# Attention feeding a mixture of experts on one core: token rows in three buffers, scatters spread over more steps, and three products of zeros

## The chip, the core and the metric

The kernel runs on one core of a Trainium2 chip. The metric is the device time of one execution in microseconds. TensorE (PE) does matmuls and transposes, VectorE (DVE), ScalarE (ACT) and GpSimd (POOL) elementwise work; POOL and SyncE (SP) issue the DMA transfers.

## What is computed

The core of the reference:

```python
scores = scale * np.matmul(q, k.transpose(0, 1, 3, 2))          # 8 batches, 8 heads, 576 positions, 64 wide
# heads 0-3: (rel >= 0) & (rel < 32); heads 4-7: (rel >= 0) & same position modulo 32
attn = softmax(np.where(masks, scores, -1e9))
x = (attn @ v) as 4608 tokens x 512
logits = x @ w_gate + modality_bias[modality_id]                # 8 experts
e_idx = np.argmax(logits, axis=1)
gate_w = probs[np.arange(N), e_idx]
for e in range(8):
    mask = e_idx == e
    h = np.maximum(x[mask] @ w1[e], 0.0)                        # 512 x 1024
    out[mask] = gate_w[mask, None] * (h @ w2[e])                # 1024 x 512
```

## The kernel before

**Attention.** The work is cut into 32 units, `Local` (one of heads 0 to 3 for two batches) and `Strided` (two of heads 4 to 7 for one batch) in turn, eight units to each pair of batches `bp` (0 to 3, 1152 tokens each). A loop over steps `n` works on several units at once: in step n it loads unit n+3, computes the scores of unit n (`s` or `ss` on PE), transposes the softmax of unit n−2 (`turn`: `t`, `ts`) and multiplies unit n−3 by its values (`values`: `o` with `vv`, `ot` with `vs`). PE's instructions stand in the order in which the code is written there. The other engines, and everything in the expert part, are ordered by a scheduler.

**Routing.** When the last unit of a pair has its values, `finish_pair` and `route` are put into the list `extra` and advanced a few pieces a step (`pop`): transposes `xl` and `xs`, logits `lg`, the chosen expert `ohb`, running counts `cum` and `cnt`, and with `rk` and `ct` on PE each token's place in a table sorted by expert. The pair's token rows `xt` (128 × 9 rows of 528 words; the last 16 hold the token's number, its gate and padding) are then written to the table `xd` in DRAM by nine indirect DMAs from POOL, the scatters `xd<-xt,posi` (L646). These stand in the list `calm`, of which each call of `slow()` issues one. `slow()` is called after the scores in odd steps, after `turn` in every step, and after `values` in odd steps. A scatter is `paced`: it waits for the matmul or transpose that was newest on PE when it was written. Behind the scatters of pair 1 stands `early()`, which fetches, one piece a call, half of slot 0's weights (`raw<-in_w`, L811), its tokens in two halves (`fx<-xd`, L792), and then the same of slot 1.

**Experts.** 18 slots of 256 tokens of one expert and a half slot follow, some 23 us each. A slot has eight parts f: the weights' high halves `wh` are cast on ACT, the low halves `wl` computed on DVE, then come 12 products `h` (`xh`, `xl` with `wh`, `wl`) and, some parts later, the products `o`; `hh` (ACT) and `hl` (DVE) stand between, `y` is the gated output on ACT. Slot 0's tokens are transposed on PE ahead of the end of the attention; those of later slots by DMA (`cols`), after which `split_tokens` copies them into order (`xs`, two copies on DVE) and makes `xh` on ACT and `xl` on DVE. In slot k the split for slot k+1 is written at part f = SPLIT = 5. In slots 0 and 1 the routing of the last pair runs along.

**Memory.** The pools `ap`, `pre` and `lp` lie on the left. `xt` has two buffers by turns, so that pair 2 writes where pair 0's rows were.

Of the kernel before, what the change touches and what calls it, by code (L numbers as in the profile page):

```python
# [11 lines left out]
F32 = mybir.dt.float32  # L12
F32R = mybir.dt.float32r
# [7 lines left out]
P = 128  # L21
# [5 lines left out]
DM = H * D  # L27
# [6 lines left out]
NSLOT = NT // SLOT + E - 1  # L34
NSTATIC = 18
ROW = DM + 16
WARM = 10
SETUP = 6, 9
POPS, MIDS, POPF = 5, 2, 2
LT, RK = 7, (10, 5)  # L40
LAG = 2
# [152 lines left out]
def attention_moe(ctx: ExitStack, tc: tile.TileContext, a, out):  # L194
# [97 lines left out]
    pre = pre_cm.__enter__()  # L292
    lp_cm = tc.tile_pool(name="lp", bufs=2, reuse_waits="tile")
    lp = lp_cm.__enter__()
    pools["lp"] = lp


# [151 lines left out]
    class Strided:  # L449
# [49 lines left out]

        def turn(self):  # L500
            n = self.n
            tp = pa(f"ts{n}").rearrange("p (g q) -> p g q", g=4)
            for g in range(4):
                turned_to(tp[0:72, g, :], self.en[:, 4 * g:4 * g + 4, :])
            self.eb = eb = lp.tile([72, 16, 4, 18], F32, tag="eb", name=f"eb{n}")
            src = tp[0:72].rearrange("p g (u x) -> p (g u) x", u=4)[:, :, 0:18]
            sh = [72, 16, 2, 18]
            nc.vector.tensor_tensor(
                eb[:, :, 0:2, :], src.unsqueeze(2).to_broadcast(sh),
                cf[0:72, C_T:C_T + 2].unsqueeze(1).unsqueeze(3).to_broadcast(sh), ALU.mult)  # L510
            for t in (2, 3):
                nc.scalar.activation(eb[:, :, t, :], src, AF.Copy, scale=cf[0:72, C_T + t:C_T + t + 1])
# [52 lines left out]
    def route(bp, xt, xcs):  # L565
# [58 lines left out]
        sm = ap.tile([P, 9], F32, tag="sml", name=f"sml{bp}")  # L624
        nc.vector.tensor_reduce(sm[:], lo[:], AX.X, ALU.add)
        nc.vector.tensor_scalar(sm[:], sm[:], 1e-9, None, ALU.add)
        nc.gpsimd.memset(xt[:, :, DM + 2:ROW], 0.0)
        paced(nc.vector.tensor_copy(xt[:, :, DM].bitcast(I32), tok[:, 9 * bp:9 * bp + 9]))
        nc.vector.reciprocal(xt[:, :, DM + 1], sm[:])

# [187 lines left out]
        return xt  # L818

    def turn_half(xt):  # L820
        xs = pre.tile([P, 4, SLOT], F32R, tag="xh", name="xhh").bitcast(F32)[:, :, 0:P]
        t = pa("xth").rearrange("p (c q) -> p c q", c=4)
        for c in range(4):
            turned_to(t[:, c, :], xt[:, 0, P * c:P * c + P])
        nc.scalar.copy(xs, t)
        le = pre.tile([P, 2, 2], I32, tag="le", bufs=4, name="leh")
        nc.vector.tensor_copy(le[:, 0, :].bitcast(U16), xt[:, 0, DM:DM + 2].bitcast(U16))
        return le, xs
# [41 lines left out]

    def turn_tokens(n, xt):

        xh = pre.tile([P, 4, SLOT], F32R, tag="xh", name=f"xh{n}")
        xl = pre.tile([P, 4, SLOT], F32R, tag="xl", name=f"xl{n}")
        for c2 in range(2):
            t = pa(f"xt{n}{c2}").rearrange("p (c h q) -> p c h q", c=2, h=2)
            for c in range(2):
                for h in range(2):
                    cc = 2 * c2 + c
                    turned_to(t[:, c, h, :], xt[:, h, P * cc:P * cc + P])  # L880
            t = t.rearrange("p c h q -> p c (h q)")
            nc.scalar.copy(xh[:, 2 * c2:2 * c2 + 2, :], t)
            nc.vector.tensor_tensor(xl[:, 2 * c2:2 * c2 + 2, :], t, xh[:, 2 * c2:2 * c2 + 2, :].bitcast(F32), ALU.subtract)
        return xh, xl, entries(n, xt)
# [17 lines left out]
    def split_tokens(fp, n, cols, le):  # L902
        xs = fp.tile([P, 4, SLOT], F32, tag="xs", bufs=1, name=f"xs{n}")
        for w in range(2):
            dst = halves(xs)[:, :, :, w].rearrange("p c (h q) -> p c h q", h=2)
            pin(nc.vector.tensor_copy(dst, cols[:, :, w].rearrange("p h c q -> p c h q")))
        xh = pre.tile([P, 4, SLOT], F32R, tag="xh", name=f"xh{n}")
        xl = pre.tile([P, 4, SLOT], F32R, tag="xl", name=f"xl{n}")
        for c0 in (0, 2):
            c = slice(c0, c0 + 2)  # L910
            nc.scalar.copy(xh[:, c, :], xs[:, c, :])  # L911
            nc.vector.tensor_tensor(xl[:, c, :], xs[:, c, :], xh[:, c, :].bitcast(F32), ALU.subtract)  # L912
        return xh, xl, le
# [52 lines left out]


    units, ends = [], {}
    for bp in range(NBP):
        xt = ap.tile([P, 9, ROW], F32, tag="xt", bufs=2, name=f"xt{bp}")  # L970
        xcs = [ap.tile([P, T2], F32, tag=f"xc{c}", bufs=1 if c < 2 else 2, name=f"xc{bp}{c}") for c in range(4)]
        for i in range(4):
            units.append(Local(bp, i, xt))
            units.append(Strided(2 * bp + i // 2, i % 2, xcs[2 + i % 2]))
        ends[len(units) - 1] = (bp, xt, xcs)
# [12 lines left out]

    def early():
        for k in range(2):  # L990
            yield
            pin(paced(weights(tables[0][1], 0, k)))
            yield
            n, t, i, xrows = plan[k]
            for xt, ins in token_halves(n, tables[t][0], i, xrows):
                gathered[k] = xt
                pin(paced(ins))
                yield

    def slow():  # L1000
        while calm and next(calm[0], calm) is calm:
# [43 lines left out]
    for n in range(nu + 3):  # L1045
        if n + 3 < nu:
            units[n + 3].load()
        if 1 <= n <= nu:
            units[n - 1].load_values()
        if 2 <= n <= nu + 1 and not n % 2:  # L1050
            units[n - 2].spread_values()
        if n < nu:
            units[n].scores()
            if n % 2:
                slow()
            pop(MIDS)
        if 2 <= n <= nu + 1:
            units[n - 2].turn()
        slow()
        if n + 1 < nu:  # L1060
            units[n + 1].masks()
        if n >= 3:
            units[n - 3].values()
            if n - 3 in ends:
                extra.append(after(*ends[n - 3]))
        if n in SETUP:
            next(setup)
        if n >= nu or n % 2:
            slow()
        pop(POPS - MIDS if n < nu else POPS)  # L1070
        if n == nu + 1:
            turn(0)
    while calm:
        slow()
# [8 lines left out]
    for k, (n, *_) in enumerate(plan):  # L1083
        def between(f):
            pop(POPF)
            if f in DRIP:
                slow()
            if k + 1 < len(plan):
                if f == SPLIT:
                    turned[k + 1] = split_tokens(fp, plan[k + 1][0], *sent[k + 1])  # L1090
            elif f == 3:
                turn(k + 1)
            if not k and not f:
                gather(2)
            if f == FETCH:
                gather(k + 3)
            for at, m in ((SEND, 2),) if k else ((1, 1), (4, 2)):
                if f == at and k + m < len(plan):
                    sent[k + m] = send_tokens(fp, plan[k + m][0], gathered[k + m])

        ffn(fp, n, *turned[k], between, partial(load, k + 1))
# [20 lines left out]

    rest(plan[-1][2] + 1)
    fp_cm.__exit__(None, None, None)
    pre_cm.__exit__(None, None, None)
    ap_cm.__exit__(None, None, None)

# [17 lines left out]
```

## Time and profile before

| | |
|---|---|
| median of 3 runs | 600.34 us (600.19 to 600.82) |
| profiled execution | 597.48 us: span 595.4, and 2.08 around it |
| mean granted TensorE clock | 0.977 |
| busy, share of the span | PE 564.8 us (95%), DVE 426.1 (72%), ACT 358.7 (60%), POOL 244.7 (41%) |
| attention, up to some 158 us | PE busy 60.14 us of the first 73, 21.02 of 73 to 98, 29.92 of 98 to 131, 25.13 of 131 to 158 |

The span is what the profiler saw on the core, from the first instruction to the last. A share of busy time is a mean over the two parts of the kernel, which have little in common; a wait is read in its own place. "issue" as the cause of a wait means that the engine waited for nothing that the profile shows.

### The profile page before, as it was taken

Reading aid. Unit: us, or ns where it says so; the run is one execution under the profiler, and the core shown is the slowest. Engines: PE = TensorE matmul, PEld = TensorE weight load, DVE = VectorE, ACT = ScalarE, POOL = GpSimd, SP = SyncE. Lnnn points to the kernel's source line nnn. Section 1 sums busy time; section 2 is a strip of 40 time slices with the busy share of each in tenths; the row PEclk is TensorE's granted clock in tenths of the full one; section 3 lists DMA queues with packets and bytes.
Section 4 is the critical chain, followed back from the end, with each engine's and each line's share of the span. In section 5 each row is a group of like instructions: output and inputs, shape, how many; then the busy total and the mean of one; then the engine's idle time right before and its main releaser. Section 6 shows DMA issues by size and latency. Waiting matters only on the chain.

```text
span 595.4 us, 15277 instructions
## 1 busy us (share of the span) xinstructions
PE 564.8 (95%) x6040; PEld 494.4 (83%) x6040; DVE 426.1 (72%) x1050; ACT 358.7 (60%) x739; POOL 244.7 (41%) x219
## 2 busy tenths in 40 slices
PE   6979888989998999999999999999999999999995
PEld 3767776767887989999899899999998998998984
DVE  6776662957969997767767777777777677677541
ACT  3455664657866566666666666665665666666641
POOL 1413240143757786642543533533534533332220
PEclk9789997989999999999999999999999999999998
DMA  8988895897788855955934823413403438200621
GB/s 275 250 220 217 250 344 189 276 341 258 262 215 210 259 164 164 236 184 129 250 119 125 248 98 74 108 36 73 109 21 87 109 119 252 71 16 22 244 91 38
DMA packets 66669, 100.57 MB, mean 169 GB/s; under 512 B 47775, under 2 KB 49055, under 8 KB 63008
## 3 DMA queue, kind: packets, MB, share of 16 engines
q0 software_dynamic: 19744, 58.57, 29.7%
q1 hardware_dynamic: 46560, 40.56, 27.0%
q8 instruction: 49, 0.80, 0.6%
q10 hardware_dynamic: 288, 0.41, 0.2%
q14 instruction: 28, 0.23, 0.1%
HBM read 121.74 MB, written 19.43 MB: 237 GB/s over the span
## 4 chain that ended last, share of the span: by engine, by line
PE 85%; issue 5%; DVE 4%; DMA 3%; ACT 2%; POOL 1%; SPq 0%; POOLq 0%; ACTq 0%
PE h L924 33%; PE o L938 32%; PE o L420 3%; PE s L380 3%; PE ot L520 3%; PE lg L571 2%; PE xs L217 2%; PE t L217 2%; PE ss L476 1%; PE xl L217 1%; PE ts L217 1%; DMA vv<-in_vb 1%; ACT wh L959 1%; DVE wl L960 1%; DMA lqk<-in_qkl 1%
## 5 line engine op out<-in xcount | busy, mean ns | idle before, releaser
L960 DVE TENSOR_TENSOR wl<-raw,wh 128x512 fp32r<-128x512 f32 x288 | 185.9, 686 | 85.0 <-ACT wh L959 84.9
L959 ACT CAST wh<-raw 128x512 fp32r<-128x512 f32 x288 | 164.0, 618 | 91.4 <-PE o L938 89.6
L924 PE MATMUL h<-xl,wh 128*128 128x256 f32 x576 | 162.1, 282 | 1.4 <-DVE xl L912 1.4
L924 PE MATMUL h<-xh,wh 128*128 128x256 f32 x576 | 163.0, 284 | 0.2 <-ACT xh L911 0.2
L924 PE MATMUL h<-xh,wl 128*128 128x256 f32 x576 | 162.8, 283 | 0.0
L811 POOL DMA_INDIRECT raw<-in_w,wi x72 | 92.7, 1287 | 162.4 <-DVE wl L960 154.1
L924 PEld LDWEIGHTS h<-xl,wh 128*128 128x128 f32 x576 | 108.8, 189 | 8.1 <-DVE xl L912 2.1
L938 PE MATMUL o<-wh,hh 128*128 128x512 f32 x288 | 114.6, 398 | 0.0
L924 PEld LDWEIGHTS h<-xh,wh 128*128 128x128 f32 x576 | 108.4, 189 | 7.1 <-issue 0.6
L938 PE MATMUL o<-wl,hh 128*128 128x512 f32 x288 | 113.6, 395 | 0.0
L938 PE MATMUL o<-wh,hl 128*128 128x512 f32 x288 | 112.2, 395 | 0.0
L924 PEld LDWEIGHTS h<-xh,wl 128*128 128x128 f32 x576 | 108.3, 188 | 0.9
L927 ACT ACTIVATE hh<-h 128x256 fp32r<-128x256 f32 x144 | 55.2, 384 | 55.0 <-PE h L924 52.7
L929 DVE SCALAR_TENSOR_TENSOR hl<-h,hh 128x256 fp32r<-128x256 f32 x144 | 60.3, 419 | 12.5 <-ACT hh L927 12.3
L646 POOL DMA_INDIRECT xd<-xt,posi x36 | 40.4, 1121 | 59.1 <-DVE sms L496 16.5
L938 PEld LDWEIGHTS o<-wh,hl 128*128 128x128 f32 x288 | 53.7, 188 | 11.8
L938 PEld LDWEIGHTS o<-wh,hh 128*128 128x128 f32 x288 | 54.3, 188 | 7.6
L938 PEld LDWEIGHTS o<-wl,hh 128*128 128x128 f32 x288 | 54.3, 189 | 5.8
L946 POOL DMA_INDIRECT out<-y,le x36 | 46.2, 1283 | 24.0 <-ACT y L945 16.1
L792 POOL DMA_INDIRECT fx<-xd,li x36 | 39.2, 1090 | 23.6 <-issue 8.5
L409 ACT COPY et<-t 64x512 f32<-64x512 f32 x32 | 18.5, 579 | 21.1 <-PE t L217 20.7
L420 PEld LDWEIGHTS o<-vv,et 128*64 128x64 f32 x512 | 19.0, 152 | 13.4 <-issue 10.1
(183 smaller groups left out, 687.9 us busy)
## 6 DMA issues: line engine op xcount, KB each, us to landing
lqk<-in_qkl SPq DMA_DIRECT2D x32, 296.0 KB
sqk<-in_qks SPq DMA_DIRECT2D x32, 288.0 KB
vv<-in_vl SPq DMA_DIRECT2D x9, 520.0 KB
vs<-in_vs SPq DMA_DIRECT2D x16, 288.0 KB
raw<-in_w,wi POOLq DMA_INDIRECT x72, 2.5
vv<-in_vb SPq DMA_DIRECT2D x7, 146.2 KB
vv<-in_vb SPq DMA_DIRECT2D x7, 130.0 KB
vv<-in_vl SPq DMA_DIRECT2D x9, 65.0 KB
```

Source lines behind the costliest of these rows:

```text
L217: recent[:] = [nc.tensor.transpose(dst, src, ident)]
L420: recent[:] = [nc.tensor.matmul(os[bb][64 * jj:64 * jj + 64, bb + k, :], et[:, 2 * (k // 2) + bb, 2 * (k % 2) + jj, :, :].rearrange("p g q ...
L646: scattered(bp, paced(nc.gpsimd.indirect_dma_start(xd[0:(bp + 1) * T2, :], IOA(ap=posi[:, i:i + 1], axis=0), xt[:, i, :], None)))
L792: yield xt, fetches(min(xrows // T2, NBP) - 1, nc.gpsimd.indirect_dma_start(xt[:, h, :], None, xd[0:xrows, :], IOA(ap=li[:, s, h:h + 1], a ...
L811: return nc.gpsimd.indirect_dma_start(raws[j].rearrange("p f c -> p (f c)"), None, a["w"], IOA(ap=wi[:, s, j:j + 1], axis=0), bounds_check ...
L924: recent[:] = [nc.tensor.matmul(hp, w[:, a1], x[:, c, :], start=(k == 0), stop=(k == 11))]
L927: nc.scalar.activation(hh[:], hp, AF.Relu)
L929: nc.vector.scalar_tensor_tensor(hl[:], hp, 0.0, hh.bitcast(F32), ALU.max, ALU.subtract)
L938: nc.tensor.matmul(os[h], hx[:, m], w[:, 512:1024], start=(f == 0 and i == 0), stop=(f == 7 and i == 2))
L946: outs.add(nc.gpsimd.indirect_dma_start(out, IOA(ap=le[:, h, 0:1], axis=0), y[:], None, bounds_check=NT - 1, oob_is_err=False))
L959: nc.scalar.copy(wh[:, c], raw[:, c])
L960: nc.vector.tensor_tensor(wl[:, c], raw[:, c], wh[:, c].bitcast(F32), ALU.subtract)
```

## The change

```diff
--- before.py
+++ after.py
@@ -34,8 +34,9 @@
 NSLOT = NT // SLOT + E - 1
 NSTATIC = 18
 ROW = DM + 16
-WARM = 10
+WARM, FILL = 10, 3
 SETUP = 6, 9
+CALM = 27
 POPS, MIDS, POPF = 5, 2, 2
 LT, RK = 7, (10, 5)
 LAG = 2
@@ -292,6 +293,8 @@
     pre = pre_cm.__enter__()
     lp_cm = tc.tile_pool(name="lp", bufs=2, reuse_waits="tile")
     lp = lp_cm.__enter__()
+    sp_cm = tc.tile_pool(name="sp", side="right")
+    sp = sp_cm.__enter__()
     pools["lp"] = lp
 
 
@@ -499,7 +502,10 @@
 
         def turn(self):
             n = self.n
-            tp = pa(f"ts{n}").rearrange("p (g q) -> p g q", g=4)
+            bank = pa(f"ts{n}")
+            for _ in range(FILL if n == 0 else 0):
+                nc.tensor.matmul(bank, idle[:, 0:P], idle[:], start=True, stop=True)
+            tp = bank.rearrange("p (g q) -> p g q", g=4)
             for g in range(4):
                 turned_to(tp[0:72, g, :], self.en[:, 4 * g:4 * g + 4, :])
             self.eb = eb = lp.tile([72, 16, 4, 18], F32, tag="eb", name=f"eb{n}")
@@ -624,7 +630,6 @@
         sm = ap.tile([P, 9], F32, tag="sml", name=f"sml{bp}")
         nc.vector.tensor_reduce(sm[:], lo[:], AX.X, ALU.add)
         nc.vector.tensor_scalar(sm[:], sm[:], 1e-9, None, ALU.add)
-        nc.gpsimd.memset(xt[:, :, DM + 2:ROW], 0.0)
         paced(nc.vector.tensor_copy(xt[:, :, DM].bitcast(I32), tok[:, 9 * bp:9 * bp + 9]))
         nc.vector.reciprocal(xt[:, :, DM + 1], sm[:])
 
@@ -818,7 +823,7 @@
         return xt
 
     def turn_half(xt):
-        xs = pre.tile([P, 4, SLOT], F32R, tag="xh", name="xhh").bitcast(F32)[:, :, 0:P]
+        xs = pools["xp"].tile([P, 4, SLOT], F32R, tag="xh", name="xhh").bitcast(F32)[:, :, 0:P]
         t = pa("xth").rearrange("p (c q) -> p c q", c=4)
         for c in range(4):
             turned_to(t[:, c, :], xt[:, 0, P * c:P * c + P])
@@ -870,8 +875,8 @@
 
     def turn_tokens(n, xt):
 
-        xh = pre.tile([P, 4, SLOT], F32R, tag="xh", name=f"xh{n}")
-        xl = pre.tile([P, 4, SLOT], F32R, tag="xl", name=f"xl{n}")
+        xh = pools["xp"].tile([P, 4, SLOT], F32R, tag="xh", name=f"xh{n}")
+        xl = pools["xp"].tile([P, 4, SLOT], F32R, tag="xl", name=f"xl{n}")
         for c2 in range(2):
             t = pa(f"xt{n}{c2}").rearrange("p (c h q) -> p c h q", c=2, h=2)
             for c in range(2):
@@ -904,8 +909,8 @@
         for w in range(2):
             dst = halves(xs)[:, :, :, w].rearrange("p c (h q) -> p c h q", h=2)
             pin(nc.vector.tensor_copy(dst, cols[:, :, w].rearrange("p h c q -> p c h q")))
-        xh = pre.tile([P, 4, SLOT], F32R, tag="xh", name=f"xh{n}")
-        xl = pre.tile([P, 4, SLOT], F32R, tag="xl", name=f"xl{n}")
+        xh = pools["xp"].tile([P, 4, SLOT], F32R, tag="xh", name=f"xh{n}")
+        xl = pools["xp"].tile([P, 4, SLOT], F32R, tag="xl", name=f"xl{n}")
         for c0 in (0, 2):
             c = slice(c0, c0 + 2)
             nc.scalar.copy(xh[:, c, :], xs[:, c, :])
@@ -966,8 +971,11 @@
 
 
     units, ends = [], {}
+    xts = [(sp if i == 1 else ap).tile([P, 9, ROW], F32, bufs=1, name=f"xt{i}") for i in range(3)]
+    for t in xts:
+        nc.gpsimd.memset(t[:, :, DM + 2:ROW], 0.0)
     for bp in range(NBP):
-        xt = ap.tile([P, 9, ROW], F32, tag="xt", bufs=2, name=f"xt{bp}")
+        xt = xts[bp % 3]
         xcs = [ap.tile([P, T2], F32, tag=f"xc{c}", bufs=1 if c < 2 else 2, name=f"xc{bp}{c}") for c in range(4)]
         for i in range(4):
             units.append(Local(bp, i, xt))
@@ -988,14 +996,13 @@
 
     def early():
         for k in range(2):
+            n, t, i, xrows = plan[k]
+            for xt, ins in token_halves(n, tables[t][0], i, xrows):
+                yield
+                gathered[k] = xt
+                pin(paced(ins))
             yield
             pin(paced(weights(tables[0][1], 0, k)))
-            yield
-            n, t, i, xrows = plan[k]
-            for xt, ins in token_halves(n, tables[t][0], i, xrows):
-                gathered[k] = xt
-                pin(paced(ins))
-                yield
 
     def slow():
         while calm and next(calm[0], calm) is calm:
@@ -1051,7 +1058,7 @@
             units[n - 2].spread_values()
         if n < nu:
             units[n].scores()
-            if n % 2:
+            if n % 2 and n >= CALM:
                 slow()
             pop(MIDS)
         if 2 <= n <= nu + 1:
@@ -1069,6 +1076,9 @@
             slow()
         pop(POPS - MIDS if n < nu else POPS)
         if n == nu + 1:
+            sp_cm.__exit__(None, None, None)
+            xp_cm = tc.tile_pool(name="xp", bufs=2, side="right", reuse_waits="tile")
+            pools["xp"] = xp_cm.__enter__()
             turn(0)
     while calm:
         slow()
@@ -1086,7 +1096,7 @@
             if f in DRIP:
                 slow()
             if k + 1 < len(plan):
-                if f == SPLIT:
+                if f == (SPLIT if k else SPLIT - 1):
                     turned[k + 1] = split_tokens(fp, plan[k + 1][0], *sent[k + 1])
             elif f == 3:
                 turn(k + 1)
@@ -1122,6 +1132,7 @@
 
     rest(plan[-1][2] + 1)
     fp_cm.__exit__(None, None, None)
+    xp_cm.__exit__(None, None, None)
     pre_cm.__exit__(None, None, None)
     ap_cm.__exit__(None, None, None)
 
```

- **CALM = 27**: the call of `slow()` after the scores falls away in odd steps before 27. An odd step then issues two scatters in place of three, an even step one as before. Pair 0's nine, which took steps 15 to 19 (1, 1, 3, 1, 3), take steps 15 to 21 (1, 1, 2, 1, 2, 1, 1); pair 1's, steps 23 to 27 before, now end in step 28 (1, 1, 2, 1, 3, 1).
- **Three buffers**: `xt` of pair bp is `xts[bp % 3]`, and only pair 3 comes back to a buffer. The padding is set three times at the start, in place of once a pair in `route`. The second buffer lies in a pool on the right, closed at step 33; the pool `xp` then opened there takes `xh` and `xl`.
- **early()**: both halves of a slot's tokens go ahead of its weights.
- **FILL = 3**: three products of zeros, 128 × 512, into the PSUM bank of the first strided transposes `ts`, ahead of them (step 3).
- **SPLIT − 1** in slot 0: slot 1's tokens are split at part 4.

On POOL, where pairs 0 and 1 are scattered and the first slots are fetched, before (the number behind a name is its buffer; 1152x528 is the part of the table that a scatter can reach):

```order
L646 DMA xd<-xt_123,posi_1415 1152x528 x9
L627 MEMSET xt_133 128x9x14
L646 DMA xd<-xt_128,posi_2163 2304x528 x9
L627 MEMSET xt_138 128x9x14
L811 DMA raw_2704<-in_w,wi_2225 128x2048
L792 DMA fx_0_2787<-xd,li_2217 128x528 x2
L811 DMA raw_2904<-in_w,wi_2225 128x2048
L792 DMA fx_1_2975<-xd,li_2217 128x528 x2
L646 DMA xd<-xt_133,posi_2979 3456x528 x6
```
After:

```order
L651 DMA xd<-xt_126,posi_1422 1152x528 x9
L651 DMA xd<-xt_127,posi_2169 2304x528 x9
L797 DMA fx_0_2710<-xd,li_2223 128x528 x2
L816 DMA raw_2863<-in_w,wi_2231 128x2048
L797 DMA fx_1_2867<-xd,li_2223 128x528 x2
L816 DMA raw_3061<-in_w,wi_2231 128x2048
L651 DMA xd<-xt_128,posi_2981 3456x528 x7
```
Both memsets between the scatters are gone, and the weights `raw` have moved from ahead of two gathers to behind them; which step a scatter belongs to these rows don't show.

On PE at step 3, after the change (`ss` are the scores of the second strided unit, `s` the mask of the next local one):

```order
L472 MATMUL ss_292<-cb_sb 128x288
L479 MATMUL ss_292<-sqk_90 18x36 x32
L507 LDWEIGHTS idle
L507 MATMUL ts_343<-idle 128x512
L507 LDWEIGHTS idle
L507 MATMUL ts_343<-idle 128x512
L507 LDWEIGHTS idle
L507 MATMUL ts_343<-idle 128x512
L218 MATMUL ts_343<-cf_sb,ens_240 72x128 x4
L371 LDWEIGHTS cb_sb
L371 MATMUL s_355<-cb_sb 128x256
```
The six rows with `idle` are new; without them the `ts` transposes followed on the `ss` products.

On DVE towards the end of slot 0, before (the first digit behind `wl_` and `hl_` is the slot by turns, the second the part f):

```order
L610 TENSOR_TENSOR ohb_3502<-cf_sb,m_3500 128x72
L960 TENSOR_TENSOR wl_11_3719<-raw_2704,wh_11_3718 128x512
L625 TENSOR_REDUCE sml_3512<-lo_3491 128x9
L614 SCALAR_TENSOR_TENSOR cum_3504<-ohb_3502 128x72
L929 SCALAR_TENSOR_TENSOR hl_07_3589<-h_07_3574,hh_07_3587 128x256
L626 TENSOR_SCALAR sml_3512<-sml_3512 128x9
L616 TENSOR_TENSOR new_3506<-cum_3504,ohb_3502 128x8
L629 RECIPROCAL xt_138<-sml_3512 128x9
L906 COPY xs_1_3518<-cols_1_3338 128x1024
L617 TENSOR_TENSOR fst<-new_3506,cnt 128x8
L906 COPY xs_1_3518<-cols_1_3338 128x1024
L960 TENSOR_TENSOR wl_12_3762<-raw_2904,wh_12_3761 128x512 x2
```
After, the stretch behind `hl_07`:

```order
L934 SCALAR_TENSOR_TENSOR hl_07_3597<-h_07_3582,hh_07_3595 128x256
L610 TENSOR_TENSOR lo_3509<-lo_3509,mxl_3513 128x72
L965 TENSOR_TENSOR wl_12_3770<-raw_3061,wh_12_3769 128x512
L612 SCALAR_TENSOR_TENSOR sc_3516<-lo_3509,cf_sb 128x72
L965 TENSOR_TENSOR wl_12_3770<-raw_3061,wh_12_3769 128x512
L614 TENSOR_REDUCE m_3518<-sc_3516 128x9
L965 TENSOR_TENSOR wl_13_3809<-raw_3061,wh_13_3808 128x512 x2
L616 TENSOR_TENSOR ohb_3520<-cf_sb,m_3518 128x72
L631 TENSOR_REDUCE sml_3530<-lo_3509 128x9
L620 SCALAR_TENSOR_TENSOR cum_3522<-ohb_3520 128x72
L632 TENSOR_SCALAR sml_3530<-sml_3530 128x9
L622 TENSOR_TENSOR new_3524<-cum_3522,ohb_3520 128x8
```
The two copies of `xs` now stand 14 rows ahead of this piece, behind `hl_04`. `ohb` stood between the two halves of `wl_11` and stands behind `wl_13` now, and with it `cum`, `fst` and `cnt` have moved behind `wl_13` and `wl_14`.

On PE at the same place, before:

```order
L938 MATMUL o_01_3379<-wl_07_3566,hh_07_3587 128x512
L638 LDWEIGHTS cb_sb
L638 MATMUL rk_3594<-cum_3504,cb_sb 128x72
L938 MATMUL o_00_3378<-wh_07_3565,hl_07_3589 128x512
L938 MATMUL o_01_3379<-wh_07_3565,hl_07_3589 128x512
L924 MATMUL h_10_3612<-xh_1_3521,wh_10_3606 128x256
L692 LDWEIGHTS cb_sb
L692 MATMUL ct_3629<-cnt,cb_sb 128x32
L692 LDWEIGHTS cb_sb
L692 MATMUL ct_3629<-stp,cb_sb 128x32
L924 MATMUL h_11_3727<-xh_1_3521,wh_11_3718 128x256
L924 MATMUL h_12_3767<-xh_1_3521,wh_12_3761 128x256
```
After:

```order
L943 MATMUL o_01_3388<-wh_07_3573,hl_07_3597 128x512
L642 LDWEIGHTS cb_sb
L642 MATMUL rk_3602<-ohb_3520,cb_sb 128x72
L929 MATMUL h_10_3620<-xh_1_3459,wh_10_3614 128x256
L929 MATMUL h_10_3620<-xl_1_3460,wh_10_3614 128x256
```
and, nine products of `h_10` later:

```order
L929 MATMUL h_10_3620<-xh_1_3459,wl_10_3615 128x256
L643 LDWEIGHTS cb_sb
L643 MATMUL rk_3602<-cum_3522,cb_sb 128x72
L697 LDWEIGHTS cb_sb
L697 MATMUL ct_3637<-cnt,cb_sb 128x32
L697 LDWEIGHTS cb_sb
L697 MATMUL ct_3637<-stp,cb_sb 128x32
L929 MATMUL h_11_3735<-xh_1_3459,wh_11_3726 128x256
```
`rk<-ohb`, which stood among the products of part 6 and 7, is now the last thing ahead of slot 1's first product, and `rk<-cum` and both `ct` stand behind all 12 products of `h_10`, where `ct` stood behind the first.

## Rows read from the trace of the kernel before

**Rows 1.** Busy time by stretch (start:end, length, engines, clock, DMA share, GB/s).
```profile
191.00:595.00 404.00, 397.60 (x2533) 359.40 (x2531) 292.73 (x582) 244.91 (x482) 173.70 (x140) 1.00 0.45 128
```

**Rows 2.** PE's waits by line: us in total, times, longest.
```profile
PE o L420 <- issue: 7.4, 3, 4.0
PE ss L476 <- issue: 3.6, 4, 1.4
...
PE s L380 <- issue: 1.6, 1, 1.6
```

**Rows 3.** PE timeline: `lg` of bp 0, then step 19.
```profile
54.25 1.93 PE L571 MATMUL lg<-xc,wg_sb 128*32 128x256 f32 x32
...
86.40 0.68 PE L420 MATMUL o<-vv,et 128*64 128x65 f32 x15
91.06 1.24 PE L420 MATMUL o<-vv,et 128*64 128x65 f32 x17 [3.98 <-issue]
...
93.86 3.63 PE L571 MATMUL lg<-xc,wg_sb 128*32 128x256 f32 x32
```

**Rows 4.** The page's DMA queues over the whole run.
```profile
q8 instruction: 49, 0.80, 0.6%
```

**Rows 5.** DMA queues (packets, MB, share) in 82:88, 88:89 and 112:118 us.
```profile
q1 hardware_dynamic: 410, 1.29, 61.9%
q0 software_dynamic: 240, 0.81, 33.3%
...
q8 instruction: 1, 0.02, 5.9%
...
q1 hardware_dynamic: 418, 1.37, 80.8%
q0 software_dynamic: 62, 0.22, 9.2%
```

**Rows 6.** PE timeline at 110, at 121 and at the tokens of slot 0.
```profile
110.02 0.57 PE L476 MATMUL ss<-sqk 128*18 128x36 f32 x43 [0.37 <-issue]
...
121.07 1.24 PE L420 MATMUL o<-vv,et 128*64 128x65 f32 x21 [1.71 <-issue]
...
122.61 1.93 PE L380 MATMUL s<-lqk 128*32 128x128 f32 x32
...
153.96 1.09 PE L217 MATMUL xt<-cf_sb,fx 128*128 128x128 f32 x8
```

**Rows 7.** Busy time by stretch in two slow stretches, columns as in Rows 1.
```profile
16.00:22.00 6.00, 4.76 (x74) 3.85 (x76) 4.26 (x11) 0.89 (x2) 2.53 (x3) 0.50 0.94 271
...
91.00:97.00 6.00, 5.94 (x62) 3.71 (x66) 1.15 (x6) 0.76 (x2) 1.05 (x1) 0.50 0.71 249
```

**Rows 8.** POOL timeline: scatters, a memset and the last early gather.
```profile
85.38 0.96 POOL L646 DMA_INDIRECT xd<-xt,posi  x1 [2.03 <-PE xl L217]
...
97.02 0.20 POOL L627 MEMSET xt<- 128x126 f32 x1 [2.92 <-DMA xd<-xt,posi]
...
149.17 0.94 POOL L792 DMA_INDIRECT fx<-xd,li  x1 [0.86 <-PE ts L217]
```

**Rows 9.** PE timeline in the first 19 us.
```profile
1.87 3.96 PE L317 MATMUL warm<-idle 128*128 128x512 bf16 x10 [1.87 <-DVE idle L313]
...
15.10 0.74 PE L217 MATMUL ts<-cf_sb,ens 128*72 128x128 f32 x4 [1.02 <-DVE ens L498]
...
18.04 1.24 PE L420 MATMUL o<-vv,et 128*64 128x65 f32 x18 [0.57 <-POOL vv L361]
```

**Rows 10.** Timelines of PE, DVE and ACT between slots 0 and 1.
```profile
190.20 0.39 PE L924 MATMUL h<-xl,wh 128*128 128x256 f32 x1 [1.40 <-DVE xl L912]
...
176.35 1.29 DVE L960 TENSOR_TENSOR wl<-raw,wh 128x512 fp32r<-128x512 f32 x2 [1.20 <-ACT wh L959]
...
179.56 1.29 DVE L894 COPY rows<-fx 128x1024 uint16<-128x1024 uint16 x2 [1.10 <-issue]
...
188.05 1.25 ACT L945 ACTIVATE y<-o,le 128x512 f32<-128x512 f32 x2
```

## The prediction

> **What bounds the kernel now.** I read four views in this order: busy time by stretch, PE's waits, the PE timeline around the longest of them, and the DMA queues there. PE is the engine that ends last. From 191 us to the end, in the expert part, it is busy 397.60 of 404.00 us at full clock [rows 1], with the end of the output behind it, so nothing is to be had there. In the attention, ahead of 158 us, it waits more and doesn't always have the full clock. So the time that a change can win lies before 191 us, as PE's idle time or as time at half clock.
>
> The list of waits names "issue" for the most of PE's idle time: 7.4 us in three waits, 3.6 in four and 1.6 in one, 12.6 us on three lines [rows 2], where no semaphore holds PE. The longest is at step 19: PE runs 15 of 32 `o` matmuls from 86.40 to 87.08, and goes on at 91.06, 3.98 us later [rows 3]. What it lacked, the DMA view suggests: a queue of kind "instruction" (q8, 49 packets, 0.80 MB in the run, so 16 KB each [rows 4]) moves nothing in 82 to 88 us, and one packet of 0.02 MB in 88 to 89, two microseconds before PE resumes [rows 5]. I read these stalls as PE waiting for its next block of instructions, which stands in the DMA engines behind data. In 82 to 88 the engines are full: loads (q1) hold 61.9%, the indirect scatters and their like (q0) 33.3%. Before the 1.71 us stall that ends at 121.07 [rows 6], in 112 to 118, q0 held 9.2% and q1 80.8% [rows 5]. The loads are there both times; the scatters tell the two apart.
>
> The stall costs twice. From 91 to 97 PE is busy 5.94 of 6.00 us at a granted clock of 0.50, the 1.2 GHz level [rows 7]: its 32 `lg` matmuls take 3.63 us, where bp 0's took 1.93 at full clock [rows 3].
>
> The Trainium skill ("Runtime: NRT & Kernel Launch", Instruction fetch mechanics) says that the sequencer fetches its next page over its own DMA queue while it runs the current one, and that crossing a 16 KiB boundary is mostly hidden. By that page these waits would be something else and fewer scatters would win nothing, which is rival B's sum. The trace agrees on the separate queue and on 16 KB a packet; it speaks against "mostly hidden".
>
> **Fewer scatters a step (CALM).** Before, an odd step issues three scatters (after scores, after turn, after values), an even step one. After, the first of the three is gone until step 27. The two left-out ones of bp 0 go to steps 20 and 21, those of bp 1 from step 25 to 28. At the stall of step 19, before, eight scatters are out, the last two issued from 85.38 on [rows 8]; after, six. The cost of an issue (0.96 us of POOL [rows 8]) doesn't change. What six in place of eight do to the stall the trace doesn't show. From below: the other stalls, with the same loads and few or no scatters, are 1.4 us at most on the `ss` line and 1.6 on the `s` line [rows 2], 1.71 at 121.07. From above: 3.98, no change. By q0's share, 33.3% would become about 25% (six eighths), and a line from (9.2%, 1.71) to (33.3%, 3.98) gives 3.2 us; but of the two that go, one (85.38) is among the four issued nearest ahead of the packet, so in the last stretch a third of the scatters or more goes, and the line gives about 2.4. I take **2.6: −1.4 us**, range −2.7 (to 1.3) to 0.
>
> **The clock behind it.** From 91.06 to about 97.4 some 6.3 us of PE work at half clock would be 3.2 at full clock. Behind the stall of 1.71 us at 121.07 the loss is short: its first 32 `s` take 1.93 us [rows 6], and the products behind them have their usual length again. So a shorter stall leaves half of the slow stretch: `lg` alone would win 3.63 − 1.93 = 1.70 [rows 3]. I take **−1.7**; bounds 0 and −3.2.
>
> **Three products of zeros (FILL).** They stand in front of the first `ts` transposes (step 3), which wait 1.02 us for DVE's `ens` (15.10) [rows 9]. Ten of the same kind took 3.96 us at 1.87 us [rows 9], so three take 1.2 at most, on an engine that waits 1.02 anyway: a cost of 0.2 at most. What they may do is keep the clock: 16 to 22 us is at 0.50, 4.76 of 6.00 busy [rows 7]. Two waits for POOL's copies of `vv` follow in it; the second ends at 18.04 [rows 9] whatever the clock is, so a full clock wins about half of 18.04 to 22.3, 2.1 us. Against it: these two waits idle PE for 1.2 us more, so the clock may fall all the same. Ends +0.2 and −2.1; with nothing in the trace nearer to the one than to the other I take **−0.9**, about the middle.
>
> **Slot 1's split one step earlier (SPLIT).** Between slots 0 and 1 PE waits 1.40 us for `xl` [rows 10], and some 0.2 each for `xh` and `cnt`. `xs` and `xl` move into two holes of DVE, 1.20 us ahead of 176.35 and 1.10 ahead of 179.56 [rows 10], 1.3 us each, so these waits go. But the routing of bp 3 then comes later: `ohb` now stands behind `wl_12` and `wl_13` on DVE, whose casts end on ACT just ahead of the `y` at 188.05, with those of `xh` no longer between; I put it at about 188.2, and PE, in front of `rk<-ohb` at 187.5, waits about 1. `cnt` stands behind `wl_14`, whose cast stands on ACT behind both `y`, 188.05 to 189.30 [rows 10], so about 190.9; PE gets there after 12 products of `h_10` (0.12 apart), near 190.0, and waits about 1 more. That ends at about 191.1 with all 12 done. Before, the wait for `xl` ended at 190.20 with 3 of them done, and nine more take until 191.3. So **−0.2**; ends −1.8 (no wait left) and +1.0 (another `wl` or two late).
>
> **At nothing.** The padding memsets: that of bp 2's rows waits 2.92 us for scatters to land [rows 8], that of bp 3's does the same later, but on POOL, with only the first weights behind, which PE needs not before the expert part at 158. The rows' third buffer removes 0.3 us of DVE's wait behind the same scatters, which no PE row shows. Early gathers ahead of weights: the last gather was issued at 149.17 [rows 8], and PE turned the tokens at 153.96 without a wait [rows 6]; after, the two halves of slot 0 come first, those of slot 1 a step or less from where they were. If bp 1's last scatter, now in step 28, held the gathers back, those 4.8 us of cover would go first.
>
> **Sum.** −1.4 −1.7 −0.9 −0.2 = −4.2 us on the profiled execution (597.48: span 595.4 and 2.08 around it) gives 593.3. That execution is 2.86 below the median of the runs, 600.34, so I forecast 600.34 − 4.2 = **596.1**.
>
> **Rivals.** Under 0.2% (1.2 us) a measurement of this kernel can hardly be told from no change.
> - **A, the sum** (0.46): 596.1, own range 593.5 to 598.5.
> - **B, the stall stays** (0.25). The block waits for loads, or for the mere presence of scatters, not for their number. For it: q1 alone holds 61.9 to 80.8% in these stretches; stalls stand where q0 moved little. Left are FILL and SPLIT: −0.9 − 0.2 = 599.2, from 598.0 to 600.3 as the clock at 16 us holds or not. The Trainium skill ("DMA: Bandwidth & Descriptors", Queues, rings and completion order) states such a rule: each DMA engine goes round the rows that have work, one packet at a time, so that a packet waits for one per other row, however many are queued. This case's one packet that came two microseconds ahead of the end of a 3.98 us stall doesn't look like it.
> - **C, everything falls into place** (0.14). The stall goes to 1.3, as where no scatters are (−2.7), the clock doesn't fall behind it (−3.2), FILL holds it at 16 us (−2.1), SPLIT −0.2: −8.2, 592.1.
> - **D, slower: the stall moves** (0.15). The two scatters of bp 0 that went to steps 20 and 21 meet the next late block there: the stall that ends at 110.02 is 0.37 us now [rows 6], with no scatters ahead of it. If it grows to 3.98 (+3.6) and takes the clock along (+3.2), it gives 600.34 − 4.2 + 6.8 = 602.9. It decides from a new stall of about 2.5 us with half of the slow stretch (1.7) behind it. Against it: one scatter a step there, and two or three issued one by one ahead of 121.07 brought 1.71.
>
> Faster by more than 0.2%: nearly all of A, half of B, C: 0.70. Within: half of B, bits of A and D: 0.16. Slower: most of D: 0.14. The range leaves out D's middle and half of C: 591.8 to 601.3.
>
> **What would show it.** In the after trace: the wait of `o<-vv,et` in step 19 (near 3.98 for B, 2 to 3 for A, 1.3 for C); the 32 `lg` behind it, 3.63 or 1.93; the first `ts` without 1.02 of idle and the clock from 16 to 22; a new issue wait in `ss` or `s` of step 21 (D); between slots 0 and 1, waits of PE for `ohb` and `cnt` in place of `xl`. I am wrong if the issue waits follow the program position whatever scatters do, or if half-clock stretches turn up in other places from execution to execution: the runs' median stands 2.86 us above this profile, and I can't say where.

## The result

| | before | changed |
|---|---|---|
| median, 20 runs each | 597.91 us (591.48 to 605.69) | 591.12 us (584.92 to 604.69) |
| ratio, 95% interval | | 0.989 [0.9859, 0.9921] |
| profiled execution: span, mean clock | 595.4, 0.977 | 589.4, 0.982 |

The change is faster by 1.1%, 6.6 us of 597.91 (4.7 to 8.4 by the interval). Forecast were 4.2 us, and 596.1 for the time; 591.12 lies 0.7 us below the range. The forecast counted from 600.34, the median of three runs; 20 runs of the same kernel have 597.91. So of the 5.0 us between 596.1 and 591.12, 2.4 are the base, and the rest is that the change won more than the sum. Single executions of one kernel spread over 14 us and more, and ratios leave disturbed runs out. The two profiles show that the sum also looked in the wrong place.

PE's waits after, us in total, times, longest; they answer to [rows 2] and [rows 10]:

```profile
PE o L423 <- issue: 4.6, 2, 2.6
PE ss L479 <- issue: 3.3, 2, 2.7
...
PE xs L218 <- ACT xc L550: 2.1, 1, 2.1
...
PE rk L642 <- DVE ohb L616: 1.8, 1, 1.8
...
PE ct L697 <- DVE cnt L628: 0.3, 1, 0.3
```

The PE timeline after, at the products of zeros, at step 19, at the stall that answers to the one at 121.07, and between slots 0 and 1:

```profile
13.97 0.82 PE L507 MATMUL ts<-idle 128*128 128x512 bf16 x3
14.96 0.63 PE L218 MATMUL ts<-cf_sb,ens 128*72 128x128 f32 x4 [0.17 <-DVE ens L501]
...
16.92 1.15 PE L423 MATMUL o<-vv,et 128*64 128x65 f32 x30 [0.72 <-POOL vv L364]
...
20.18 1.22 PE L526 MATMUL ot<-eb,vs 72*64 72x72 f32 x32
...
90.07 0.80 PE L423 MATMUL o<-vv,et 128*64 128x65 f32 x20 [1.92 <-issue]
...
92.38 2.87 PE L577 MATMUL lg<-xc,wg_sb 128*32 128x256 f32 x32
...
119.27 0.92 PE L423 MATMUL o<-vv,et 128*64 128x65 f32 x24 [2.64 <-issue]
...
187.70 0.19 PE L642 MATMUL rk<-ohb,cb_sb 128*128 128x72 bf16 x1 [1.76 <-DVE ohb L616]
...
189.79 0.19 PE L697 MATMUL ct<-cnt,cb_sb 128*128 128x32 bf16 x1 [0.34 <-DVE cnt L628]
```

Step 19 stalls for 1.92 where it stalled for 3.98 [rows 3], and the `lg` behind it take 2.87 where they took 3.63. But step 25 stalls for 2.64 where it stalled for 1.71 [rows 6]. And by the first products of slot 1 little has been won: behind the first 12 of them, and `ct` with its wait, PE goes on at 189.85, where behind the first 12 it was 191.37, 1.5 us later. The windows after show where the rest came, in the same columns as [rows 1] and [rows 7].

```profile
16.00:22.00 6.00, 5.28 (x182) 4.54 (x182) 4.55 (x14) 2.28 (x5) 0.86 (x1) 1.00 0.99 259
91.00:97.00 6.00, 6.00 (x97) 3.84 (x89) 1.78 (x6) 1.82 (x4) 0.96 (x1) 0.72 0.86 280
191.00:589.00 398.00, 391.76 (x2521) 356.42 (x2519) 289.16 (x575) 244.36 (x481) 163.31 (x138) 1.00 0.46 132
```

In the expert part PE is as full as before (391.76 of 398.00), at full clock, and done 6.0 us of span earlier. The gated outputs `y` of slots 2, 3 and 9 on ACT, before:

```profile
237.63 1.38 ACT L945 ACTIVATE y<-o,le 128x512 f32<-128x512 f32 x2 [0.26 <-PE o L938]
260.31 1.38 ACT L945 ACTIVATE y<-o,le 128x512 f32<-128x512 f32 x2 [0.26 <-PE o L938]
...
396.35 1.38 ACT L945 ACTIVATE y<-o,le 128x512 f32<-128x512 f32 x2 [0.25 <-PE o L938]
```

After:

```profile
235.63 1.37 ACT L950 ACTIVATE y<-o,le 128x512 f32<-128x512 f32 x2 [0.24 <-PE o L943]
258.04 1.37 ACT L950 ACTIVATE y<-o,le 128x512 f32<-128x512 f32 x2 [0.25 <-PE o L943]
...
392.48 1.37 ACT L950 ACTIVATE y<-o,le 128x512 f32<-128x512 f32 x2 [0.25 <-PE o L943]
```

Six slots from 260.31 to 396.35 are 22.673 us each; from 258.04 to 392.48 they are 22.407. From slot 2's `y` to the end of the span it is 357.8 before (595.4 − 237.63) and 353.8 after: 4.0 of the 6.0 us, in a stretch where the same products run in the same number. Two us (in this pair of profiles) remain for all that the prediction summed.

### The profile page after: what moved, and what is told of

Its sections match the earlier page's. It is cut to its first block, busy times and chain, and to the rows that moved or that the text cites. A ratio compares the mean times of both kernels' runs of the same rounds, so it can differ in the third digit from the quotient of the medians.

```text
span 589.4 us, 15281 instructions
## 1 busy us (share of the span) xinstructions
PE 558.5 (95%) x6043; PEld 491.2 (83%) x6043; DVE 421.5 (72%) x1050; ACT 357.8 (61%) x739; POOL 235.7 (40%) x218
## 4 chain that ended last, share of the span: by engine, by line
PE 83%; DMA 5%; issue 4%; DVE 3%; ACT 2%; POOL 1%; SPq 1%; POOLq 0%; DVEq 0%; ACTq 0%
PE h L929 34%; PE o L943 33%; PE s L383 2%; PE o L423 2%; DMA vv<-in_vb 2%; DMA lqk<-in_qkl 2%; DMA raw<-in_w,wi 2%; PE ot L526 2%; PE lg L577 2%; PE xs L218 1%; PE xl L218 1%; PE t L218 1%; PE ss L479 1%; PE ts L218 1%; ACT wh L964 1%
## 5 line engine op out<-in xcount | busy, mean ns | idle before, releaser
L816 POOL DMA_INDIRECT raw<-in_w,wi x72 | 84.4, 1172 | 161.1 <-DVE wl L965 155.9
L943 PE MATMUL o<-wh,hh 128*128 128x512 f32 x288 | 113.2, 393 | 0.0
L423 PEld LDWEIGHTS o<-vv,et 128*64 128x64 f32 x512 | 17.7, 144 | 12.4 <-issue 7.0
```

Source lines behind the costliest of these rows:

```text
L423: recent[:] = [nc.tensor.matmul(os[bb][64 * jj:64 * jj + 64, bb + k, :], et[:, 2 * (k // 2) + bb, 2 * (k % 2) + jj, :, :].rearrange("p g q ...
L816: return nc.gpsimd.indirect_dma_start(raws[j].rearrange("p f c -> p (f c)"), None, a["w"], IOA(ap=wi[:, s, j:j + 1], axis=0), bounds_check ...
L943: nc.tensor.matmul(os[h], hx[:, m], w[:, 512:1024], start=(f == 0 and i == 0), stop=(f == 7 and i == 2))
```

## The experiments

Two numbers are read from each profile: the slot's length as above, and the stretch from slot 2's `y` to the end. "Before" is the median of the kernel before, measured on the same chip together with the run.

| kernel | slot us | to the end us | median us | before us | ratio, 95% |
|---|---|---|---|---|---|
| e0_before | 22.673 | 357.1 | 599.99 | 600.0 | 1.0067 [1.0016, 1.0117] |
| e1_only_buffers | 22.407 | 353.4 | 592.93 | 600.0 | 0.9943 [0.9889, 0.9997] |
| e2_all_but_buffers | 22.673 | 357.2 | 600.37 | 600.0 | 1.0047 [0.9998, 1.0096] |
| e3_only_calm | 22.673 | 357.1 | 608.57 | 600.0 | 1.0127 [1.0053, 1.0201] |
| e4_after | 22.407 | 353.8 | 598.45 | 601.01 | 0.9953 [0.9911, 0.9994] |
| e5_after_no_calm | 22.407 | 353.8 | 595.92 | 601.01 | 0.9916 [0.9879, 0.9954] |
| e6_after_no_fill | 22.407 | 354.2 | 596.80 | 601.01 | 0.9952 [0.9917, 0.9987] |
| e7_after_no_split | 22.407 | 353.2 | 598.77 | 601.01 | 0.9929 [0.9885, 0.9974] |
| p1_xp_32_lower | 22.673 | 357.4 | 600.1 | 602.8 | one run |
| p2_before_fp_right | 22.453 | 355.1 | 603.13 | 602.8 | one run |
| p3_before_pad32 | 22.673 | 357.4 | 605.03 | 602.8 | one run |
| p4_before_xh32 | 22.553 | 355.4 | 595.99 | 598.22 | 0.999 [0.9938, 1.0043] |
| p5_after_xh64 | 22.673 | 357.2 | 593.52 | 598.22 | 0.9949 [0.9911, 0.9987] |
| v1_after_hh32 | 22.520 | 355.0 | 592.52 | 598.22 | 0.9938 [0.9896, 0.9979] |
| v2_before_xh32_hh32 | 22.610 | 356.3 | 598.47 | 598.22 | 1.0035 [0.9993, 1.0077] |
| p6_after | 22.407 | 353.3 | 589.48 | 598.66 | 0.9884 [0.984, 0.9927] |
| p7_after_xh64 | 22.673 | 357.5 | 593.06 | 598.66 | 0.9953 [0.9916, 0.9989] |
| p8_buffers_xh64 | 22.673 | 357.2 | 595.20 | 598.66 | 0.9994 [0.9949, 1.0038] |

e0 is the kernel before against itself, and its interval misses 1, though the medians agree (599.99 and 600.0). So a ratio of this table is not read closer than 0.007; the slot's length repeats to 0.01 us in the three programs that have more than one profile.

**Which part.** e0 has no edit. e1 has the three buffers alone:

```diff
-        xt = ap.tile([P, 9, ROW], F32, tag="xt", bufs=2, name=f"xt{bp}")
+        xt = xts[bp % 3]
...
-        nc.gpsimd.memset(xt[:, :, DM + 2:ROW], 0.0)
...
-        xh = pre.tile([P, 4, SLOT], F32R, tag="xh", name=f"xh{n}")
+        xh = pools["xp"].tile([P, 4, SLOT], F32R, tag="xh", name=f"xh{n}")
```

e2 has every other line of the change and none of these; e3 has only this one:

```diff
-            if n % 2:
+            if n % 2 and n >= CALM:
                 slow()
```

> The kernel before itself, once more, for a second profile of it. Three theories on the 6.0 us by which the span of the profiled execution fell, of which some 4 came behind 191 us, where a slot of the expert part takes 22.67 us before and 22.41 after. Attention theory (the prediction's): the change wins in the attention and at the first slots alone, and the length of a slot is chance; it differs between executions of one kernel. Placement theory: the length of a slot belongs to the kernel, by where its tiles lie in memory. Here: attention theory, a slot off 22.67 by 0.1 us or more; placement theory, 22.65 to 22.70. Time: ratio 1.00 to itself.

> The kernel before with the three buffers alone (padding at the start, rows in three buffers, xh and xl in the pool on the right). Placement theory: a slot of 22.41 us, ratio about 0.993 (18 slots by 0.26 us, 4.7 us). Attention theory: a slot as long as that of the kernel before on this chip within 0.1, ratio 0.999 to 1.001; the stall of step 19 and the half clock behind it as before.

> All of the change but the three buffers: fewer scatters a step, early gathers first, products of zeros, the earlier split; rows in two buffers, padding in the routing, xh and xl where they were. Attention theory: the whole gain, ratio 0.985 to 0.993. Placement theory: a slot of 22.67 us, and only what the attention wins, ratio 0.995 to 0.998. Both: the stall of step 19 at 2 to 3 us.

> Fewer scatters a step alone. Prediction's reading: the stall of step 19 falls to 1.9 to 2.6 us, the lg behind it from 3.63 to 2.9 or less, ratio about 0.995 (3.1 us). Rival B (the block waits for loads, whatever the scatters do): the stall stays above 3.5, ratio 1.00.

The attention theory falls for the slot: it is 22.673 in e0, e2 and e3 and 22.407 in e1. e1 gains (0.9943, where the whole change has 0.9953 in e4 and 0.9884 in p6, on other chips); e2 gains nothing. And e3 is slower than before, by 8.6 us of the medians. In e3 the waits of DVE for the pair's rows, and PE's wait behind them:

```profile
106.93 1.55 DVE L447 TENSOR_TENSOR xt<-o,rs 128x256 f32<-128x256 f32 x4 [2.16 <-DMA xd<-xt,posi]
...
139.74 0.82 DVE L447 TENSOR_TENSOR xt<-o,rs 128x256 f32<-128x256 f32 x2 [3.50 <-DMA xd<-xt,posi]
```

```profile
PE ot L521 <- DVE xt L447: 2.3, 1, 2.3
```

Pair 2's rows go into pair 0's buffer, and pair 0's last scatter is issued at 101.81 in e3, where it was issued at 93.05 before. With two buffers, spreading the scatters holds DVE up; with three (after) it has no such wait. e2, with CALM and two buffers too, has the same waits (DVE 3.00 and 3.49, PE 3.1 behind the first) and is no slower than before, so they are not all of e3's 8.6 us. What e3 has and e2 has not is a late slot 1: its tokens are fetched behind the weights, at 151.15 and 153.09 us (in e2 at 145.70 and 147.66), and DVE and PE wait for them.

```profile
188.92 1.30 DVE L895 COPY rows<-fx 128x1024 uint16<-128x1024 uint16 x2 [6.54 <-DMA fx<-xd,li]
```

```profile
192.02 0.73 PE L939 MATMUL o<-wh,hl 128*128 128x512 f32 x2 [3.13 <-DVE hl L930]
...
198.89 0.58 PE L925 MATMUL h<-xl,wh 128*128 128x256 f32 x1 [2.23 <-DVE xl L913]
```

So CALM needs the buffers, and by this pair of profiles perhaps the new order in `early()` too. That isn't shown: e2 also has FILL and the earlier split, p4 waits 4.49 us for these tokens without CALM, and no run has CALM and the buffers with the old order.

In e0 step 19 stalls for 2.11 us, without a change to anything:

```profile
88.84 0.74 PE L420 MATMUL o<-vv,et 128*64 128x65 f32 x17 [2.11 <-issue]
91.09 2.86 PE L571 MATMUL lg<-xc,wg_sb 128*32 128x256 f32 x32
...
117.81 1.35 PE L420 MATMUL o<-vv,et 128*64 128x65 f32 x21 [2.81 <-issue]
```

**Taking parts back from the change**: CALM = 0 (e5), FILL = 0 (e6), and in e7

```diff
-                if f == (SPLIT if k else SPLIT - 1):
+                if f == SPLIT:
```

> The changed kernel once more, on the chip on which its parts are taken back. Ratio to before 0.987 to 0.992 by either theory; a slot of 22.41 us in this execution too if the slot belongs to the placement of the tiles.

> The change with three scatters in odd steps again (CALM = 0). The prediction's sum: 3.1 us slower than the change, ratio to before about 0.005 higher, and a stall of 3 us or more in step 19 with a longer slow stretch behind it. Buffers theory (the three buffers and the shorter slot are the whole gain): the same ratio as the change within 0.003, the slot 22.41.

> The change without the three products of zeros. The prediction's sum: 0.9 us slower than the change, by its own bounds 0 to 2.1; buffers theory: the same within 0.003. Half clock from 16 to 22 us comes back if the products hold it.

> The change with slot 1's split at part 5. The prediction's sum: 0.2 us slower, not to be told by time; in the profile PE's waits between slots 0 and 1 go back from ohb and cnt (about 2 us) to xl, xh and cnt (about 1.8).

None is slower than the change beside it (e4) by what time can tell; without CALM it is 2.5 us faster by the medians, less than their spread, where the sum wanted 3.1 slower. The step-19 stall doesn't follow CALM: 1.86 us in e5 with three scatters, at a full clock behind it (`lg` 1.93):

```profile
85.59 0.57 PE L423 MATMUL o<-vv,et 128*64 128x65 f32 x12
88.02 0.80 PE L423 MATMUL o<-vv,et 128*64 128x65 f32 x20 [1.86 <-issue]
...
89.70 1.93 PE L577 MATMUL lg<-xc,wg_sb 128*32 128x256 f32 x32
```

Over all 20 profiles: nine without CALM have this wait at 1.49 to 3.98, median 1.86, and 3.98 is the one that the prediction was read from (the next is 2.39). Of eleven with CALM nine have it at 0.70 to 2.53, median 1.85, and two wait at the `ot` before it instead (2.53 and 2.10). Some profiles wait at both; together the two waits have medians of 2.66 without CALM and 2.20 with it, in ranges that overlap (1.86 to 3.98 and 2.03 to 3.29).

What the wait does follow is the place in the program. It stands behind 15 of the 32 `o` products in every profile without FILL that has it (15 in [rows 3]; 17 behind it in e0), and behind 12 in every one with FILL (e5 above), where three products more stand ahead. Counted over PE's instructions that is the 3776th to 3780th in all 18. The wait at the `ot` ahead of it lies 256 instructions earlier, that of step 25 five times 256 later; of the 105 "issue" waits of 0.6 us and more in the first 165 us of the 20 profiles, every one lies at a multiple of 256 instructions from there, to within four. And every one ends 1.2 to 1.7 us after a 16 KB packet of the queue of kind "instruction" has landed; that queue has 49 packets [rows 4], and PE's 6040 weight loads and 6040 matmuls are 47 times 256. So the reading of these waits as blocks of instructions that come late is borne out; which of them comes late, and by how much, changes from execution to execution, and the number of scatters doesn't show in it.

The products of zeros mostly do what was hoped of them: without them (e6) 16 to 22 us is partly at half clock again.

```profile
16.00:22.00 6.00, 5.10 (x91) 4.26 (x92) 4.23 (x13) 0.97 (x3) 1.22 (x3) 0.72 1.01 265
```

The first `ot` products (20.18 above; 23.19 before) begin at 19.93 to 23.19 us, median 22.27, in the ten profiles without FILL, and at 19.81 to 21.70, median 20.18, in the ten with it. The clock of 16 to 22 us is 1.00 in nine of the ten with it and in two of the ten without (e0 and p8). At pair 0's `lg`, near 51 us, 1.8 of these 2.1 us are left (medians 52.54 and 50.70). At pair 1's, near 91, it is 0.7, less than the spread. e6's time shows nothing of it.

e7's waits between the slots went back to `xl` (1.4) and `xh` (0.4), as expected.

**Where the tiles lie.** In the built program before, the four tiles of `xh` and `xl` begin at multiples of 64 bytes within a partition, as do `wh`, `wl`, `hh` and `hl`. The change's pool on the right puts `xh` and `xl` 32 bytes beyond one, and the expert part's pool `fp` 16 KB lower. p1 to p3 move them. p1 is the change with a gap of 32 bytes behind `xh` and `xl`, which moves them down and leaves all other tiles of a slot, and the instructions of every engine, as they were:

```diff
             turn(0)
+            pools["xp"].tile([P, 8], F32, bufs=1, name="gap")
```

p2 is the kernel before with `fp` on the right, p3 the kernel before with the same gap ahead of everything in `pre`:

```diff
-    fp_cm = tc.tile_pool(name="fp", bufs=2, reuse_waits="tile")
+    fp_cm = tc.tile_pool(name="fp", bufs=2, side="right", reuse_waits="tile")
```

```diff
     pools["lp"] = lp
+    pre.tile([P, 8], F32, bufs=1, name="gap")
```

> The change with xh and xl 32 bytes lower in their pool (their addresses a multiple of 64 as before the change, where the change put them at 32 beyond one); all else where the change has it. If that offset shortens the slot: back to about 22.67 us. If the distance between tiles or the 16 KB by which the expert part's other tiles moved down does it: 22.41.

> The kernel before with the expert part's pool (weights, hh, hl, xs) on the right, which moves its tiles up by 1440 bytes to 32 beyond a multiple of 64; xh and xl stay. If what counts is that the two operands of a product differ by 32 modulo 64: 22.41 us, as after the change. If what counts is the address of xh and xl alone, or the 16 KB: 22.67.

> The kernel before with 32 bytes of padding ahead of all tiles of the expert part, so that xh, xl and the weights all move by 32. If the difference of 32 between operands counts: 22.67 us. If the address of xh and xl alone counts: 22.41.

p1, the change with 32 bytes of difference:

```profile
263.43 1.38 ACT L950 ACTIVATE y<-o,le 128x512 f32<-128x512 f32 x2 [0.26 <-PE o L943]
...
399.47 1.38 ACT L950 ACTIVATE y<-o,le 128x512 f32<-128x512 f32 x2 [0.25 <-PE o L943]
```

22.673 again, to the last digit. p3, all 32 beyond: 22.673. p2, `fp` 32 beyond and `xh`, `xl` not: 22.453. So it looked as if the difference between the operands counts, and not the address of one.

p4 sets the difference in the kernel before, with two gaps of 32 bytes around `xh` and `xl` (together they move `fp` up by 64); p5 is p1's kernel, timed:

```diff
+    pre.tile([P, 8], F32, bufs=1, name="gap")
...
+            pre.tile([P, 8], F32, bufs=1, name="gap1")
```

v1 (on the change) and v2 (on p4) also move `hh` and `hl`, which stand against the weights in the products `o`, and what lies behind them in `fp`:

```diff
+                pools["gap"] = fp.tile([P, 8], F32, bufs=1, name="gaph")
```

> The kernel before with two gaps of 32 bytes in its memory alone: xh and xl lie 32 bytes off the weights modulo 64, everything else as before. Address theory (a slot is 22.67 us when the operands of the products h lie alike modulo 64 and 22.41 when they lie 32 apart, and the change's gain is that): slot 22.41, ratio to before 0.990 to 0.995 (17 slots by 0.266 us, 4.5 us). If the third buffer itself is needed: 22.41 in the slot and a ratio above 0.996.

> The change with xh and xl 32 bytes lower, so that they lie as the weights do modulo 64; the kernel of p1_xp_32_lower, now timed. Address theory: slot 22.67 us, ratio to before 0.997 to 1.003. The prediction's sum (stall, clock, products of zeros, split): 0.993.

> The change with a gap of 32 bytes ahead of hh and hl, so that in the products o the two operands lie 32 apart modulo 64 too. Address theory carried on: o products of about 229 us per thousand fall by 2 to 4 ns each, a slot of 22.2 to 22.3 us, 2 to 3 us less than the change. Rival: only h is concerned, or the step from h to o pays it back: 22.41 or more.

> The kernel before with the three gaps alone (xh and xl, and hh and hl, 32 bytes off the weights modulo 64). Address theory: the slot of v1_after_hh32, and a ratio to before lower than that of p4_before_xh32 by 0.003 to 0.005 if that slot is 22.2 to 22.3 us.

The rule "32 apart is 22.41" falls here: p4 has 22.553, half of it, and v1, which ought to have been shorter than the change, 22.520. Where the tiles lie sets the slot's length, but by more than these 32 bytes. And p5, with its long slot, had the ratio of e4 with its short one, which the address theory can't have. The last three runs stand side by side on one chip. p8 is e1 with p1's gap.

> The change itself, beside the next two on one chip. The stretch from the gated output of slot 2 to the end takes 353.2 to 354.2 us in every profile with slots of 22.41 us and 357.1 to 357.8 with slots of 22.67; here 353 to 354. Address theory: about 4 us less than p7_after_xh64. If the address gains nothing in total because the time ahead of it makes up for it: the same as p7_after_xh64 within 1.5 us.

> The kernel of p5_after_xh64 again: the change with xh and xl lying like the weights modulo 64. Address theory: 4 us more than p6_after, and what the other parts win or lose ahead of slot 2 shown against the kernel before: ratio 0.997 to 1.000. If p5_after_xh64's ratio (0.995) was no chance: 0.993 to 0.996.

> The kernel before with the three buffers alone and xh and xl lying like the weights modulo 64: what the buffers win by themselves, without the address. Slots of 22.67 us. If they win nothing ahead of slot 2: ratio 1.000 within 0.002; if they are what helps there (no memset and no row waits for scatters): 0.993 to 0.997, and no difference from p7_after_xh64 if the other parts win nothing.

589.48 against 593.06 us: the 32 bytes are worth 3.6 us in the total (1.8 to 5.0 by the spread of the runs), 4.2 by the stretch to the end (353.3 and 357.5). That p5 and e4 came out alike is within what two chips at different times leave open. Without the address the change still has 0.9953, as p5 had 0.9949; each is within 0.007 of 1, but the two agree. The buffers alone without it have 0.9994, though their median is 3.5 us below that of the kernel before, and 2.1 us above p7's; what they win by themselves these runs don't tell.

## Why the prediction was wrong

- **The step that failed first** is "so nothing is to be had there", on the expert part. PE was busy there for 397.60 of 404.00 us, and I took busy for fixed. The same products take 1.2% less in other places of memory: 4.0 of the 6.0 us between the profiles, 3.6 us in p6 against p7. It came with an edit, `xh` and `xl` in another pool, that the part "At nothing" didn't even price. No row of the profile before shows such a price; the addresses could have been read, the effect not.
- **The base** is the other part of the miss: from 600.34 the measured 6.6 us would have come to 593.7, inside the range. The three runs lay within 0.6 us of each other, the 20 within 14.2.
- **CALM's −1.4 and the clock's −1.7** were sized on one execution. 3.98 us was the longest step-19 stall of nine; the usual one is 1.86 with three scatters and 1.85 with two, and with the wait at `ot` ahead of it the medians differ by 0.5 us: nearer to rival B than to A. The working leaned the same way: with a third of the scatters gone its line gives 2.9, and the 2.4 that it names wants half of them gone. Both signs that it named for being wrong came true: the waits follow the program position, and half clock turns up elsewhere in other executions (in e0 the granted clock is 0.50 from 120 to 123 and from 192 to 195 us). The slow stretch behind it (`lg` over 3.5 us) turned up in three of nine profiles without CALM and in one of eleven with it, too few to tell. That a block of instructions is late is borne out; what the late blocks wait for, no run has shown.
- **"The rows' third buffer removes 0.3 us"** holds before the change only. With CALM and two buffers DVE waits 2.16 and 3.50 us (e3), and e3, in which slot 1's tokens came late too, is 1.3% slower. That is the slower rival that I should have had. D, a new stall in step 21, was not seen: the profile after has no issue wait there, and 0.5 us in step 24; the wait at 110.02 that D started from stands in step 23.
- **FILL −0.9** was the right mechanism at less than half its size: the upper bound, −2.1, is what the first `ot` show. Some of that seems to be given back on the way to 91 us, and the total shows none of it (e6).
- **SPLIT −0.2**: waits of 1 and 1 for `ohb` and `cnt` were forecast, 1.76 and 0.34 measured; `xl` is gone from the list. Time can't tell the net.
- **The sum**: p7, the change without the address, is the kernel that the prediction thought it had: ratios of 0.9949 (p5, the same kernel) and 0.9953, 3.1 and 2.8 us, near the 4.2. It agrees with the sum, and not with its terms; that is luck. Which parts bring it stays open between the buffers and the rest together (p8 to p7), and e5 to e7 take none of it back alone.

## What to carry to other kernels

Where PE was full here, its time still depended on where the operands lie: after an edit that moves pools, compare the length of a steady slot first, which two profiles give to 0.01 us, before any story about waits. Take no term from one stall of one execution: a second profile of the unchanged kernel costs little, and here it showed 2.11 us in place of 3.98. Take no base from three runs because they agree. An edit that delays the readers of a buffer has to be priced together with the number of buffers. And before a wait is put down to what runs beside it, see whether it stands at the same instruction in another profile.

## What was not expected of the hardware

The pace of PE's products depends on the places of their operands in on-chip memory: with the same products on data of the same type a slot took 22.673, 22.610, 22.553, 22.520, 22.453 or 22.407 us, by kernel, and the same again where a kernel has more than one profile (22.407 in three of the change, 22.673 in two of the kernel before and in three of p1's). Moving `xh` and `xl` alone by 32 bytes is worth 0.266 us (p1), and moving `hh`, `hl` and what lies behind them by 32 costs 0.113 (v1). What in the memory makes the difference the runs don't show.

In this kernel PE's "issue" waits stand at every 256th of its instructions (105 of 105 of 0.6 us and more, up to 165 us in 20 profiles), and end 1.2 to 1.7 us after a 16 KB packet of the instruction queue. The largest were 3.98 us (before) and 3.56 us (v2).
